# Four edits to the opening of a two-layer transformer kernel: order of weight rows, DMA transposes, finer evacuation, passes of 128 tokens

## Chip, cores, metric

One core of a Trainium2 chip. The metric is the device time of one execution in microseconds (us). The fast runs of one kernel in one group of rounds lie within 0.03 to 0.25% of each other; times are compared within rounds on one chip, fast runs only (one run of the kernel before took 3484 us and is not fast). "TensorE", "vector engine" (DVE), "ACT" and "sync engine" (SP) are the engines; SP does nothing here but issue DMAs.

## The reference

Two layers, each of attention and a gated MLP, on 2048 tokens of 1024 features in bf16:

```python
x = x + attention(layernorm(x), wqkv, wo)   # 32 heads of 32; 8 keys per token, 2 apart
x = x + w2( silu(w1 ln(x)) * (w3 ln(x)) )   # F = 3584
# and both once more with the same weights
```

`attention` projects Q, K and V by one matrix `wqkv` (1024 x 3072), gathers keys and values at 0, 2, ..., 14 tokens back, takes a softmax over 8 logits, and projects by `wo`.

## The kernel before

Tokens are worked in 4 chunks of 512. TensorE runs: Q of chunk 0 (the opening, `first_q`), K and V of chunk 0, then Q, K, V of chunks 1 to 3, with the first tiles of the output projection between the products of chunk 3, then the rest of the output projection and the MLP chunk by chunk. Attention itself has no product: the vector engine does it elementwise from transposed Q, K, V, which go through DRAM (`qkv_d`). It works in halves of 256 tokens, and its output `oT` is what the output projection takes.

The opening: x arrives in tiles of 128 tokens, is normalised, transposed by TensorE through PSUM, and multiplied by wq, which arrives in 8 rows of 256 KB. All DMAs but one are issued on the sync engine, in this order:

```python
load_tile(0, 0, 512, nc.sync);  load_tile(0, 512, D, nc.scalar)   # x tile 0
load_tile(1, 0, D, nc.sync)
loads(0, 2);  load_tile(2, 0, D, nc.sync)      # rows 0,1 of wq; x tile 2
loads(2, 4);  load_tile(3, 0, D, nc.sync)      # rows 2,3; x tile 3
loads(4, 8)          # rows 4..7, then (k1 == KT) both halves of wk and x chunk 1: 3 MB
# ... cut: statistics, normalisation, transposes, products of the four tiles
for i, acc in enumerate(accumulators(2, 2 * P)):     # tiles 2 and 3: one pass of 256 columns
    ...
    nc.sync.dma_start(q_rows[:, 2 * i:2 * i + 2, 0:CH], hT[:, 2 * i:2 * i + 2, :])  # Q to DRAM
    then[i]()        # x chunk 2; half of wv; other half of wv; x chunk 3
```

The K pass that follows, cut:

```python
for t0 in range(0, KT, SG):                       # SG = 2
    sgt = stg.tile([P, SG, CH], BF16, name="sgt") # 3 buffers
    for t in range(t0, t0 + SG):
        ...8 products of 512 columns into ps...
        background(r)                             # vector engine's work, in a fixed order
        nc.scalar.copy(sgt[:, t - t0, :], ps[:])  # ACT
    nc.sync.dma_start(qkv_d[l][which][:, t0:t0 + SG, c * CH:(c + 1) * CH], sgt[:])
```

The order of instructions on each engine is fixed when the kernel is built (in c1 below the vector engine stands idle for 2.68 us before statistics that are ahead of attention in that order). The square root of each norm is an ACT instruction between those copies, and the vector engine waits for it (6 waits, 6.1 us in all, between 20 and 165 us of the profile before):

```python
nc.vector.bn_aggr(mv[:, i, :], st[:, i, :, :])
if i == 1:
    nc.scalar.activation(sd[:], mv[:, :, 1], ACTF.Sqrt, bias=epst[:])
...
yield 0.10, at["sd"], lambda: nc.vector.reciprocal(rstd[:], sd[:])
```

And the vector engine's order is: norm of x chunk 1, statistics of x chunks 2 and 3, then attention without a break.

Of the kernel before, what the change touches and what calls it, by code (L numbers as in the profile page):

```python
# [7 lines left out]
FP32 = mybir.dt.float32  # L8
BF16 = mybir.dt.bfloat16
# [6 lines left out]
def kernel(  # L16
# [13 lines left out]
    nc = tc.nc  # L30
    cfg = dict(cfg or {})
    P = 128
    _, S, D = A_x.shape
    F = B_w1.shape[1]
    KT = D // P
    W, DIL, Dh = 8, 2, 32
    assert D == 1024 and KT == 8 and D // Dh == 32
    CH = 512
    NCH = S // CH
    TPC = CH // P  # L40
# [35 lines left out]
    psum = ctx.enter_context(tc.tile_pool(name="psum", bufs=8, space=PSUM))  # L76
# [70 lines left out]
    ident = const.tile([P, P], BF16, name="ident")  # L147
# [13 lines left out]
    hT = const.tile([P, HTN, CH], BF16, name="hT")  # L161
# [3 lines left out]
    def warm(n):  # L165
        for i in range(n):
            pw = bank("pw")
            nc.tensor.matmul(pw[:], lhsT=zero[:, 0, 0:P], rhs=zero[:, 0:2, :].rearrange("p a b -> p (a b)"),
                             start=True, stop=True)
# [8 lines left out]
    KH = KT // 2  # L178
# [51 lines left out]
    def first_q(ws, loads, then):  # L230


        xnT = xnTs["Q", 0, 0] = xtp.tile([P, KT, CH], BF16, name="xnT")
        st = small.tile([P, TPC, 2, 6], FP32, name="st1", bufs=1)
        mv = small.tile([P, TPC, 2], FP32, name="mv1", bufs=1)
        sd = small.tile([P, TPC], FP32, name="sd1", bufs=1)
        rstd = small.tile([P, TPC], FP32, name="rstd1", bufs=1)
        q_rows = qkv_d[0][0][:].rearrange("i t s -> (i t) s").rearrange("(b p) s -> p b s", p=P)

        def load_tile(j, h0, h1, queue):  # L240
            queue.dma_start(x_sb[:, j, h0:h1], xin[:, j, h0:h1])  # L241

        load_tile(0, 0, 512, nc.sync)
        load_tile(0, 512, D, nc.scalar)
        load_tile(1, 0, D, nc.sync)
        loads(0, 2)
        load_tile(2, 0, D, nc.sync)
        loads(2, 4)
        load_tile(3, 0, D, nc.sync)
        loads(4, 8)  # L250
        preload = small.tile([P, 1], FP32, name="preload", bufs=1)
        nc.scalar.activation(preload[:], epst[:], ACTF.Sqrt)

        def stats(j, hh):
            nc.vector.bn_stats(st[:, j, hh, :], x_sb[:, j, hh * 512:(hh + 1) * 512])  # L255

        def deviation(j):
            nc.vector.bn_aggr(mv[:, j, :], st[:, j, :, :])
            nc.scalar.activation(sd[:, j:j + 1], mv[:, j, 1:2], ACTF.Sqrt, bias=epst[:])  # L259

        def apply(j, parts=1):
            nc.vector.reciprocal(rstd[:, j:j + 1], sd[:, j:j + 1])
            xn = xnp.tile([P, D], BF16, name="xn")
            for i in range(parts):
                d = slice(i * D // parts, (i + 1) * D // parts)
                nc.vector.tensor_scalar(xn[:, d], x_sb[:, j, d], mv[:, j, 0:1], rstd[:, j:j + 1],  # L266
                                        op0=ALU.subtract, op1=ALU.mult)
            return xn

        def transpose(xn):  # L270
            pTs = []
            for h in range(2):
                pT = psum.tile([P, KH, P], BF16, name="pT", tag="mm")
                for kk in range(KH):
                    nc.tensor.transpose(pT[:, kk, :], xn[:, (h * KH + kk) * P:(h * KH + kk + 1) * P], ident[:])  # L275
                pTs.append(pT)
            return pTs

        def evacuate(j, h, pTs, copy):
            copy(xnT[:, h * KH:(h + 1) * KH, j * P:(j + 1) * P], pTs[h][:])  # L280

        def product(out, kk, b, tok, start, stop):
            nc.tensor.matmul(out, lhsT=ws[kk // KH][:, kk % KH, b * P:(b + 1) * P], rhs=xnT[:, kk, tok],  # L283
                             start=start, stop=stop, skip_group_check=True)

        def accumulators(per, n):
            return [psum.tile([P, per, n], FP32, name="pq", tag="mm") for _ in range(KT // per)]

        warm(NWARM)
        stats(0, 0)  # L290
        stats(0, 1)
        deviation(0)
        stats(1, 0)
        xn = apply(0, 2)
        pTs = transpose(xn)
        evacuate(0, 0, pTs, nc.scalar.copy)
        stats(1, 1)
        evacuate(0, 1, pTs, nc.vector.tensor_copy)
        deviation(1)

        accs = accumulators(4, P)
        tok = slice(0, P)

        def step0(kk):
            for b in range(KT):
                product(accs[b // 4][:, b % 4, :], kk, b, tok, kk == 0 and b % 4 == 0, kk == KT - 1)

        for kk in range(6):
            step0(kk)
        stats(2, 0)  # L310
        xn = apply(1)
        pTs = transpose(xn)
        for h in range(2):
            evacuate(1, h, pTs, nc.scalar.copy)
        for kk in range(6, KT):
            step0(kk)
        stats(2, 1)
        deviation(2)
        for i in range(2):
            nc.scalar.copy(hT[:, 4 * i:4 * i + 4, tok], accs[i][:])  # L320

        accs = accumulators(4, P)
        tok = slice(P, 2 * P)

        def block1(b):
            for kk in range(KT):
                product(accs[b // 4][:, b % 4, :], kk, b, tok, kk == 0, kk == KT - 1)
            if b % 4 == 3:
                nc.scalar.copy(hT[:, b - 3:b + 1, tok], accs[b // 4][:])

        stats(3, 0)
        xn = apply(2)
        stats(3, 1)
        deviation(3)
        for b in range(3):
            block1(b)
        pTs = transpose(xn)
        for h in range(2):
            evacuate(2, h, pTs, nc.scalar.copy)
        xn = apply(3)  # L340
        for b in range(3, 5):
            block1(b)
        pTs = transpose(xn)
        evacuate(3, 0, pTs, nc.scalar.copy)
        evacuate(3, 1, pTs, nc.vector.tensor_copy)
        for b in range(5, KT):
            block1(b)

        tok = slice(2 * P, CH)
        for i, acc in enumerate(accumulators(2, 2 * P)):  # L350
            for b in range(2):
                for kk in range(KT):
                    product(acc[:, b, :], kk, 2 * i + b, tok, kk == 0, kk == KT - 1)
            nc.scalar.copy(hT[:, 2 * i:2 * i + 2, tok], acc[:])
            nc.sync.dma_start(q_rows[:, 2 * i:2 * i + 2, 0:CH], hT[:, 2 * i:2 * i + 2, :])
            then[i]()
        qkv_at[0, 0, 0] = now["act"] + DMA / 2

    def tree(n, mul, dst):
# [144 lines left out]
    w_tiles, due, used = [], [], [0]  # L504

    def load_weight(pieces=1):

        if len(w_tiles) == len(seq):
            return
        kind, i, n, *rest = seq[len(w_tiles)]  # L510
        if kind == "qkv":
            w = wp.tile([P, KH, D], BF16, name="wqkv", tag="w")
            step = KH // pieces
            for k0 in range(0, KH, step):
                nc.sync.dma_start(w[:, k0:k0 + step, :],
                                  wqkv_v[:, n * KH + k0:n * KH + k0 + step, i * D:(i + 1) * D])
        elif kind == "w2":
            w = wp.tile([P, 8, 512], BF16, name="w2t", tag="w")
            nc.sync.dma_start(w[:, 0:n, :], w2_v[:, i:i + n, rest[0] * 512:(rest[0] + 1) * 512])
        else:  # L520
            w = wp.tile([P, KT, FG * P], BF16, name=kind + "t", tag="w")
            v = w1_v if kind == "w1" else w3_v
            nc.sync.dma_start(w[:, :, 0:n * P], v[:, :, i * P:(i + n) * P])
        w_tiles.append(w)
# [151 lines left out]
    def load_x(c):  # L676
        nc.sync.dma_start(x_sb[:, c * TPC:(c + 1) * TPC, :], xin[:, c * TPC:(c + 1) * TPC, :])
# [3 lines left out]
    def load_wq(k0, k1):  # L681
        for kk in range(k0, k1):
            nc.sync.dma_start(w_tiles[kk // KH][:, kk % KH, :], wqkv_v[:, kk, 0:D])  # L683
        if k1 == KT:
            load_weight()
            load_weight()
            load_x(1)

    first_q(w_tiles[0:2], load_wq, (lambda: load_x(2), load_weight, load_weight, lambda: load_x(3)))
    xnT_at["Q", 0, 0], norm_left["Q", 0, 0] = now["pe"], 0  # L690
    queue_norm(("Q", 0, 1), 1, 0)
    queue_norm(("Q", 0, 1), 1, 1)
# [3 lines left out]
    for c in range(NCH):  # L696
        for which in range(3):
# [4 lines left out]
            then = ()  # L702
            if c == 0 and which == 0:
                continue
            if c == 2 and which == 0:
                then = (None, None, lambda: nc.sync.dma_start(wo[:], wo_v))
            if c == 2 and which == 1:
                then = (load_weight, None, load_weight)
# [50 lines left out]
```

## Time and profile before

| | before |
|---|---|
| median of 6 runs (lowest fast) | 1618.8 us (1618.17) |
| span in the profile | 1616.3 us |
| first product of the K pass | 24.64 us |
| first attention instruction on the vector engine | 47.74 us |
| last `oT` of the first 512 tokens starts | 160.38 us |

From the page of the kernel before: span, busy time of each engine, granted TensorE clock in 40 slices (9 means 0.9 or more), and the shares of the chain of waits that ended last.

```profile
span 1616.3 us, 19263 instructions
...
PE 1610.7 (100%) x7609; PEld 805.3 (50%) x7609; DVE 1176.6 (73%) x1965; ACT 353.6 (22%) x547; POOL 1.9 (0%) x12
...
PEclk9999999999999999999999999999999999999999
...
PE 99%; DMA 0%; SPq 0%; DVE 0%; ACT 0%; issue 0%
```

TensorE is busy for the whole span, and nearly the whole chain is TensorE.

The 3 MB of wk and x chunk 1 are issued by 8.9 us. At 37.16 the first stores of K are issued. On the sync engine they stand behind two DMA transposes of x chunk 1, which both kernels have, and the issue of these ends at 37.06, about when the last load ahead of them, x chunk 3, has landed (37.18). ACT waits 3.48 us for the first of the stores, because it has to free a buffer of `sgt`; the square root behind ACT's copy (40.51) then ends a wait of 2.29 us of the vector engine (40.85). At 159.32 TensorE begins the output projection's tile that reads the last parts of `oT`, and the last part is written at 160.38 to 160.67. Below "waits", for all time after 25 us, stands this one line for TensorE (us in total, times, longest):

```profile
PEld L552 <- DVE oT L371: 0.2, 1, 0.2
```

A note on times: from here on, landings, those of the prediction too, are counted from a zero 0.12 us later than that of the timelines. The landing of x chunk 3 at 37.18 on the timelines is 37.06 there.

### The profile page before, as it was taken

Reading aid. Unit: us, or ns where it says so; the run is one execution under the profiler, and the core shown is the slowest. Engines: PE = TensorE matmul, PEld = TensorE weight load, DVE = VectorE, ACT = ScalarE, POOL = GpSimd, SP = SyncE. Lnnn points to the kernel's source line nnn. Section 1 sums busy time; section 2 is a strip of 40 time slices with the busy share of each in tenths; the row PEclk is TensorE's granted clock in tenths of the full one; section 3 lists DMA queues with packets and bytes.
Section 4 is the critical chain, followed back from the end, with each engine's and each line's share of the span. In section 5 each row is a group of like instructions: output and inputs, shape, how many; then the busy total and the mean of one; then the engine's idle time right before and its main releaser. Section 6 shows DMA issues by size and latency. Waiting matters only on the chain.

```text
span 1616.3 us, 19263 instructions
## 1 busy us (share of the span) xinstructions
PE 1610.7 (100%) x7609; PEld 805.3 (50%) x7609; DVE 1176.6 (73%) x1965; ACT 353.6 (22%) x547; POOL 1.9 (0%) x12
## 2 busy tenths in 40 slices
PE   9999999999999999999999999999999999999999
PEld 6666544444445544455444554445544444444444
DVE  5999898989899899998998449983599832222212
ACT  4433311212112230222302123021230212011110
POOL 0000000000000000000000000000000000000000
PEclk9999999999999999999999999999999999999999
DMA  9565855466537773577553776528684266436440
GB/s 314 149 190 158 254 178 169 129 193 190 170 105 236 222 203 125 169 208 249 160 186 120 211 239 175 186 97 259 210 223 158 93 194 170 143 108 218 157 130 27
DMA packets 336427, 285.82 MB, mean 177 GB/s; under 512 B 69712, under 2 KB 318928, under 8 KB 336208
## 3 DMA queue, kind: packets, MB, share of 16 engines
q1 hardware_dynamic: 336192, 284.46, 58.0%
q8 instruction: 59, 0.97, 0.2%
q14 instruction: 32, 0.26, 0.0%
q10 hardware_dynamic: 144, 0.13, 0.0%
HBM read 239.47 MB, written 29.36 MB: 166 GB/s over the span
## 4 chain that ended last, share of the span: by engine, by line
PE 99%; DMA 0%; SPq 0%; DVE 0%; ACT 0%; issue 0%
PE acc L658 24%; PE pu L642 24%; PE pg L634 24%; PE ps L591 20%; PE po L552 7%; PE pq L283 1%; DMA wqkv<-in_A_wqkv_dram 0%; SPq L683 0%; SPq L241 0%; DVE xn L266 0%; ACT xnT L280 0%; PE pT L275 0%; DVE st L255 0%; ACT sd L259 0%; DVE x_sb L668 0%
## 5 line engine op out<-in xcount | busy, mean ns | idle before, releaser
L642 PE MATMUL pu<-xnT,w3t 128*128 128x512 bf16 x1792 | 423.4, 379 | 0.0
L634 PE MATMUL pg<-xnT,w1t 128*128 128x512 bf16 x1792 | 423.4, 379 | 0.0
L658 PE MATMUL acc<-w2t,hT 128*128 128x512 bf16 (+1 forms) x1804 | 389.7, 378 | 0.0
L591 PE MATMUL ps<-xnT,wqkv 128*128 128x512 bf16 x1472 | 319.2, 379 | 0.0
L638 ACT ACTIVATE sg<-pg 128x512 bf16<-128x512 f32 x224 | 133.6, 597 | 773.0 <-PE pg L634 719.4
L646 DVE TENSOR_TENSOR hT<-sg,pu 128x512 bf16<-128x512 bf16 x224 | 152.6, 681 | 186.8 <-PE pu L642 177.8
L658 PEld LDWEIGHTS <-hT 128*128 128x128 bf16 x1804 | 176.5, 98 | 210.5
L642 PEld LDWEIGHTS <-w3t 128*128 128x128 bf16 x1792 | 175.4, 98 | 211.4
L634 PEld LDWEIGHTS <-w1t 128*128 128x128 bf16 x1792 | 175.3, 98 | 211.4
L591 PEld LDWEIGHTS <-wqkv 128*128 128x128 bf16 x1472 | 211.1, 143 | 106.7
L424 DVE TENSOR_TENSOR pr<-qT,kT 128x2048 bf16<-128x2048 bf16 x128 | 156.2, 1221 | 87.2 <-DMA kT<-qkv_d 85.1
L668 DVE TENSOR_TENSOR x_sb<-x_sb,acc 128x512 bf16<-128x512 bf16 x129 | 87.3, 677 | 107.6 <-PE acc L658 107.4
L484 DVE TENSOR_TENSOR tm<-At,vT 128x2048 bf16<-128x2048 bf16 x128 | 156.1, 1220 | 2.4
L595 ACT CAST sgt<-ps 128x512 bf16<-128x512 f32 x184 | 106.7, 585 | 230.7 <-PE ps L591 211.9
L369 DVE TENSOR_TENSOR tm<-tm 128x1024 bf16<-128x1024 bf16 (+1 forms) x256 | 134.5, 550 | 0.4
L369 DVE TENSOR_TENSOR pr<-pr 128x1024 bf16<-128x1024 bf16 (+1 forms) x256 | 134.0, 551 | 0.5
L552 PE MATMUL po<-wo,oT 128*128 128x512 bf16 x512 | 115.7, 379 | 0.0
L552 PEld LDWEIGHTS <-oT 128*128 128x128 bf16 x512 | 50.1, 98 | 60.1 <-DVE oT L371 0.2
L189 DVE BATCH_NORM_STATS2 st<-x_sb 128x6 f32<-128x512 bf16 x120 | 75.9, 671 | 4.6 <-DMA x_sb<-in_A_x_dram 4.6
L557 DVE TENSOR_TENSOR x_sb<-x_sb,po 128x512 bf16<-128x512 bf16 x64 | 43.3, 684 | 19.2 <-PE po L552 18.9
L638 ACT ACT_TABLE_LOAD x31 | 39.8, 1283 | 51.2 <-PE pg L634 51.0
L446 DVE STREAM_TRANSPOSE psmT<-psm 128x2048 bf16<-128x2048 bf16 x16 | 36.9, 2306 | 0.2
(85 smaller groups left out, 402.3 us busy)
## 6 DMA issues: line engine op xcount, KB each, us to landing
w1t<-in_B_w_dram SPq DMA_DIRECT2D x56, 1024.0 KB, 5.5
w3t<-in_B_w_dram SPq DMA_DIRECT2D x56, 1024.0 KB, 8.0
w2t<-in_B_w_dram SPq DMA_DIRECT2D x48, 1024.0 KB, 5.4
wqkv<-in_A_wqkv_dram SPq DMA_DIRECT2D x28, 1024.0 KB, 6.8
qkv_d<-sgt SPq DMA_DIRECT2D x92, 256.0 KB, 2.9
qT<-qkv_d SPq DMA_DIRECT2D x16, 512.0 KB, 8.4
w2t<-in_B_w_dram SPq DMA_DIRECT2D x16, 512.0 KB, 5.2
kT<-qkv_d SPq DMA_DIRECT2D x14, 544.0 KB, 9.5
```

Of the source, the lines that this page charges most:

```text
L369: nc.vector.tensor_tensor(b[:, 0:m, :], b[:, 0:m, :], b[:, m:2 * m, :], op=ALU.add)
L424: V.tensor_tensor(pr[:], qT[:], kT[:, :, k0:k0 + TCH], op=ALU.mult)
L484: V.tensor_tensor(tm[:], At[:], win, op=ALU.mult)
L552: nc.tensor.matmul(ps[:], lhsT=oT[:, t, j * P:(j + 1) * P], rhs=wo[:, t, hh * 512:(hh + 1) * 512], start=(t == 0), stop=(t == KT - 1))
L591: nc.tensor.matmul(ps[:], lhsT=ws[kk // KH][:, kk % KH, t::KT], rhs=xnT[:, kk, :], start=(kk == 0), stop=(kk == KT - 1))
L595: nc.scalar.copy(sgt[:, t - t0, :], ps[:])
L634: nc.tensor.matmul(pg[:], lhsT=w1t[:, kk, fi * P:(fi + 1) * P], rhs=xnT[:, kk, :], start=(kk == 0), stop=(kk == KT - 1))
L638: nc.scalar.activation(sg[:], pg[:], ACTF.Silu)
L642: nc.tensor.matmul(pu[:], lhsT=w3t[:, kk, fi * P:(fi + 1) * P], rhs=xnT[:, kk, :], start=(kk == 0), stop=(kk == KT - 1))
L646: nc.vector.tensor_tensor(hT[:, f - f0, :], sg[:], pu[:], op=ALU.mult)
L658: nc.tensor.matmul(acc[:], lhsT=hT[:, f - f0, j * P:(j + 1) * P], rhs=w2ts[(f - f0) // 8][:, (f - f0) % 8, q0:q0 + step], start=(f == f0), ...
L668: nc.vector.tensor_tensor(xs, xs, acc[:], op=ALU.add)
```

## The change

Its intent is to start the products of the opening sooner and keep TensorE free of transposes:

1. rows of wq load ahead of x tiles 2 and 3;
2. tiles 2 and 3 are transposed by DMA, not by TensorE and ACT;
3. the first tile's transposes are evacuated in pieces of 2, 2 and 4 blocks instead of 4 and 4;
4. tiles 2 and 3 are multiplied in two passes of 128 columns instead of one of 256.

The loads of wk and x chunk 1 move with it: they are now issued inside tile 1's pass, which on the sync engine is behind both DMA transposes.

```diff
         load_tile(1, 0, D, nc.sync)
-        loads(0, 2)
+        loads(0, 4)
         load_tile(2, 0, D, nc.sync)
-        loads(2, 4)
+        loads(4, 8)
         load_tile(3, 0, D, nc.sync)
-        loads(4, 8)
 ...
+        def transpose_dma(j, xn):
+            nc.sync.dma_start_transpose(out=xnT[:, :, j * P:(j + 1) * P], in_=xn[:])
 ...
-        pTs = transpose(xn)
-        evacuate(0, 0, pTs, nc.scalar.copy)
+        p0, p1, p2 = transpose(xn, (0, 2, 4, 8))
+        evacuate(0, p0, nc.scalar.copy)
+        evacuate(0, p1, nc.scalar.copy)
 ...
+        transpose_dma(2, xn)
 ...
+        transpose_dma(3, xn)
+
+        for j in range(1, TPC):
+            for i, acc in enumerate(accumulators()):
+                for b in range(4):
+                    for kk in range(KT):
+                        product(j, acc[:, b, :], kk, 4 * i + b, kk == 0)
+                keep(j, i, acc)
+                if j == 1 and i == 0:
+                    then[0]()                  # wk, x chunk 1
+                if j == TPC - 1:
+                    nc.sync.dma_start(q_rows[:, 4 * i:4 * i + 4, 0:CH], hT[:, 4 * i:4 * i + 4, :])
+                    then[1 + i]()              # x chunk 2, wv; wv, x chunk 3
 ...
-        if k1 == KT:
-            load_weight()
-            load_weight()
-            load_x(1)
```

More of the change, by code (lines that the diff above doesn't have):

```diff
@@ L268, in apply, with transpose, evacuate, product @@
             return xn
-        def transpose(xn):
+        def transpose(xn, cuts):
             pTs = []
-            for h in range(2):
-                pT = psum.tile([P, KH, P], BF16, name="pT", tag="mm")
-                for kk in range(KH):
-                    nc.tensor.transpose(pT[:, kk, :], xn[:, (h * KH + kk) * P:(h * KH + kk + 1) * P], ident[:])
-                pTs.append(pT)
-            return pTs
-        def evacuate(j, h, pTs, copy):
-            copy(xnT[:, h * KH:(h + 1) * KH, j * P:(j + 1) * P], pTs[h][:])
-        def product(out, kk, b, tok, start, stop):
-            nc.tensor.matmul(out, lhsT=ws[kk // KH][:, kk % KH, b * P:(b + 1) * P], rhs=xnT[:, kk, tok],
-                             start=start, stop=stop, skip_group_check=True)
-        def accumulators(per, n):
-            return [psum.tile([P, per, n], FP32, name="pq", tag="mm") for _ in range(KT // per)]
+            for k0, k1 in zip(cuts, cuts[1:]):
+                pT = psum.tile([P, k1 - k0, P], BF16, name="pT", tag="mm")
+                for kk in range(k0, k1):
+                    nc.tensor.transpose(pT[:, kk - k0, :], xn[:, kk * P:(kk + 1) * P], ident[:])
+                pTs.append((k0, k1, pT))
+            return pTs
+        def evacuate(j, part, copy):
+            k0, k1, pT = part
+            copy(xnT[:, k0:k1, j * P:(j + 1) * P], pT[:])
+        def transpose_dma(j, xn):
+            nc.sync.dma_start_transpose(out=xnT[:, :, j * P:(j + 1) * P], in_=xn[:])
+        def product(j, out, kk, b, start):
+            nc.tensor.matmul(out, lhsT=ws[kk // KH][:, kk % KH, b * P:(b + 1) * P],
+                             rhs=xnT[:, kk, j * P:(j + 1) * P], start=start, stop=kk == KT - 1,
+                             skip_group_check=True)
+        def accumulators():
+            return [psum.tile([P, 4, P], FP32, name="pq", tag="mm") for _ in range(2)]
+        def keep(j, i, acc):
+            nc.scalar.copy(hT[:, 4 * i:4 * i + 4, j * P:(j + 1) * P], acc[:])
         warm(NWARM)
@@ L294, in first_q @@
         xn = apply(0, 2)
-        pTs = transpose(xn)
-        evacuate(0, 0, pTs, nc.scalar.copy)
+        p0, p1, p2 = transpose(xn, (0, 2, 4, 8))
+        evacuate(0, p0, nc.scalar.copy)
+        evacuate(0, p1, nc.scalar.copy)
         stats(1, 1)
-        evacuate(0, 1, pTs, nc.vector.tensor_copy)
+        evacuate(0, p2, nc.vector.tensor_copy)
         deviation(1)
-        accs = accumulators(4, P)
-        tok = slice(0, P)
-        def step0(kk):
-            for b in range(KT):
-                product(accs[b // 4][:, b % 4, :], kk, b, tok, kk == 0 and b % 4 == 0, kk == KT - 1)
@@ L308, in first_q @@
-        for kk in range(6):
-            step0(kk)
         stats(2, 0)
         xn = apply(1)
-        pTs = transpose(xn)
-        for h in range(2):
-            evacuate(1, h, pTs, nc.scalar.copy)
-        for kk in range(6, KT):
-            step0(kk)
         stats(2, 1)
         deviation(2)
-        for i in range(2):
-            nc.scalar.copy(hT[:, 4 * i:4 * i + 4, tok], accs[i][:])
-        accs = accumulators(4, P)
-        tok = slice(P, 2 * P)
-        def block1(b):
-            for kk in range(KT):
-                product(accs[b // 4][:, b % 4, :], kk, b, tok, kk == 0, kk == KT - 1)
-            if b % 4 == 3:
-                nc.scalar.copy(hT[:, b - 3:b + 1, tok], accs[b // 4][:])
+        accs = accumulators()
@@ L331, in first_q @@
+        for kk in range(KT):
+            for b in range(KT):
+                product(0, accs[b // 4][:, b % 4, :], kk, b, kk == 0 and b % 4 == 0)
+            if kk == 4:
+                p0, p1 = transpose(xn, (0, 4, 8))
+        evacuate(1, p0, nc.scalar.copy)
+        evacuate(1, p1, nc.scalar.copy)
         stats(3, 0)
         xn = apply(2)
+        transpose_dma(2, xn)
         stats(3, 1)
         deviation(3)
-        for b in range(3):
-            block1(b)
-        pTs = transpose(xn)
@@ L338, in first_q @@
-        for h in range(2):
-            evacuate(2, h, pTs, nc.scalar.copy)
-        xn = apply(3)
-        for b in range(3, 5):
-            block1(b)
-        pTs = transpose(xn)
-        evacuate(3, 0, pTs, nc.scalar.copy)
-        evacuate(3, 1, pTs, nc.vector.tensor_copy)
-        for b in range(5, KT):
-            block1(b)
-        tok = slice(2 * P, CH)
-        for i, acc in enumerate(accumulators(2, 2 * P)):
-            for b in range(2):
-                for kk in range(KT):
-                    product(acc[:, b, :], kk, 2 * i + b, tok, kk == 0, kk == KT - 1)
-            nc.scalar.copy(hT[:, 2 * i:2 * i + 2, tok], acc[:])
-            nc.sync.dma_start(q_rows[:, 2 * i:2 * i + 2, 0:CH], hT[:, 2 * i:2 * i + 2, :])
-            then[i]()
+        for i in range(2):
+            keep(0, i, accs[i])
@@ new lines, in first_q @@
+        xn = apply(3)
+        transpose_dma(3, xn)
+        for j in range(1, TPC):
+            for i, acc in enumerate(accumulators()):
+                for b in range(4):
+                    for kk in range(KT):
+                        product(j, acc[:, b, :], kk, 4 * i + b, kk == 0)
[5 more added lines that the diff above has]
+                    then[1 + i]()
@@ L683, in load_wq, with load_k, load_v0, load_v1 @@
             nc.sync.dma_start(w_tiles[kk // KH][:, kk % KH, :], wqkv_v[:, kk, 0:D])
-        if k1 == KT:
-            load_weight()
-            load_weight()
-            load_x(1)
-    first_q(w_tiles[0:2], load_wq, (lambda: load_x(2), load_weight, load_weight, lambda: load_x(3)))
+    def load_k():
+        load_weight()
+        load_weight()
+        load_x(1)
+    def load_v0():
+        load_x(2)
+        load_weight()
+    def load_v1():
+        load_weight()
+        load_x(3)
+    first_q(w_tiles[0:2], load_wq, (load_k, load_v0, load_v1))
     xnT_at["Q", 0, 0], norm_left["Q", 0, 0] = now["pe"], 0
```

## The prediction

> **What bounds it now.** TensorE. The page has PE busy 1610.7 of a 1616.3 us span (100%), clock 1.000, and the chain of waits that ended last is 99% PE. The list of waits after 25 us shows 0.2 us of PE waiting in all: once the first 128x512 product of the K pass starts (24.64 us, timeline) TensorE streams without a hole for 1591.7 us. The change touches only what comes before: its worth is the shift of that start, plus any new hole. Two per cent (32 us) exceeds the whole prologue.
>
> **The prologue before** (timeline, chain of waits). First transposes at 6.28, first product 7.35 behind a 0.58 us evacuation of 512 columns on ACT. The first tile's pass is paced by rows of wq: holes of 0.24, 0.87 and 0.23 us on the weight load, each ended by a wq DMA. From the records of landings, pieces of 256 KB land about 0.66 us apart in issue order: row 3 at 8.8, row 4 at 10.1, row 7 at 12.1. The tile's pass ends near 12.7, tile 1's with the transposes of tiles 2 and 3 (about 0.45 us of PE each, plus 0.29 waiting for xn) near 17.7, then 64 products of 256 columns at 0.109 us = 7.0 us.
>
> The gap of warm products[...]: 0.056 us at 128 columns, 0.216 at 512 in this trace.
>
> **What the change does** (estimates from those durations).
> - Finer evacuation: the first copy is 256 columns (0.38 us as the cast of that size on ACT) after two transposes instead of four: first product at about 7.05, -0.3. Row 4 of wq then paces the pass: mostly lost in a wait.
> - Rows ahead of x tiles: rows 4 to 7 land one slot (0.66 us) earlier, row 7 at about 11.4. x tile 2 lands at 8.8 instead of 7.1, and its statistics stand ahead of tile 1's normalisation on DVE: xn of tile 1 at 10.3, its transposes wait about 0.3. Tile 0 ends near 12.1. The sqrt for tile 2 stands ahead of tile 1's evacuations on ACT: another 0.2-0.3 us hole. Tile 1 ends near 16.0, with no transposes inside it: 1.7 us ahead of before.
> - DMA transposes: x tile 3 still lands at 12.1; its first statistics, then xn of tile 2 at 13.65. A DMA transpose takes 1.29 us to issue and at least 3.1 (median 3.3) from issue to landing, so tile 2 is ready at about 16.9. TensorE waits about 1 us. Tile 3 (18.9) is in time.
> - Passes of 128 tokens: 128x0.056 = 7.2 instead of 7.0, +0.2.
> The K pass starts at about 24.2 instead of 24.64.
>
> **What it may cost.** The loads of wk and x chunk 1 now queue behind the transposes on the sync engine: issued at 17.0 instead of 7.3, wk's second half lands at about 24-24.6 (2.7 us per MB); it is needed at 25.0. wv's second half lands near 37.6, needed at 38.9. Either can make a hole of up to 1 us; expected 0.2.
>
> **Predicted:** 1618.4 us (-0.3), range 1616.9 to 1619.9; faster by 2% 0.005, within 0.985, slower 0.01.
>
> **Right or wrong, in the profile:** first product near 7.05; tile 0's products ending near 12.1; a TensorE wait of 1 us before tile 2's products, ended by the DMA transpose; first 128x512 product at 24.2.
>
> **What would make it wrong:** a DMA transpose quicker than 3.1 us in the quiet queue (gain up to 1 us more); wk landing behind the transposes by 1-2 us (loss); a slow run (3484 us).

The spacings are measured: 56 ns from start to start at 128 columns, 109 at 256 and 216 at 512 (medians in the profile before). The forecast's sum: 0.44 us gained at the start of the K pass (24.2 instead of 24.64), 0.2 expected to be lost in holes, recorded as -0.3 and 1618.4 us.

## More of the kernel before

The timeline of the kernel before (start, duration, engine, line, operation, output<-input, count, and in brackets how long the engine idled and what ended it):

```profile
7.25 1.32 SPq L515 DMA_DIRECT2D wqkv<-in_A_wqkv_dram  x2
8.90 0.37 SPq L677 DMA_DIRECT2D x_sb<-in_A_x_dram  x1
...
21.57 1.29 DVE L189 BATCH_NORM_STATS2 st<-x_sb 128x6 f32<-128x512 bf16 x2 [4.56 <-DMA x_sb<-in_A_x_dram]
...
24.64 35.56 PE L591 MATMUL ps<-xnT,wqkv 128*128 128x512 bf16 x164
...
26.94 10.12 SPq L217 DMA_TRANSPOSE xnT<-xn  x2
37.16 1.04 SPq L600 DMA_DIRECT2D qkv_d<-sgt  x2
...
39.76 0.59 ACT L595 CAST sgt<-ps 128x512 bf16<-128x512 f32 x1 [3.48 <-DMA qkv_d<-sgt]
...
40.51 0.31 ACT L194 ACTIVATE sd<-mv,epst 128x2 f32<-128x2 f32 x1
...
40.85 0.17 DVE L201 RECIPROCAL rstd<-sd 128x2 f32<-128x2 f32 x1 [2.29 <-ACT sd L194]
...
47.74 1.21 DVE L424 TENSOR_TENSOR pr<-qT,kT 128x2048 bf16<-128x2048 bf16 x1
...
159.32 3.62 PE L552 MATMUL po<-wo,oT 128*128 128x512 bf16 x16
...
160.38 0.29 DVE L371 TENSOR_TENSOR oT<-tm 128x256 bf16<-128x256 bf16 x1
```

## The result

| | before | after |
|---|---|---|
| median (6 runs each) | 1618.8 us | 1626.68 us |
| ratio of fast runs | | 1.0047 (95%: 1.0033 to 1.0061) |
| span in the profile | 1616.3 | 1624.3 |
| mean granted clock | 1.000 | 0.998 |
| first K product | 24.64 | 23.86 |
| K pass runs without a hole from | 24.64 | 26.36 |
| first attention instruction | 47.74 | 54.02 |
| last `oT` of the first 512 tokens starts | 160.38 | 166.66 |

A ratio is the mean time of one kernel's fast runs over that of the other's in the same rounds, so it is not quite the ratio of the medians quoted. The change is 8 us slower: within 2%, but clear of noise and far outside the predicted range. From the page of the kernel after:

```profile
span 1624.3 us, 19357 instructions
...
PE 1613.1 (99%) x7657; PEld 805.9 (50%) x7657; DVE 1176.5 (72%) x1964; ACT 350.5 (22%) x545; POOL 1.9 (0%) x12
...
PEclk9999999999999999999999999999999999999999
...
PE 90%; DVE 8%; DMA 2%; SPq 0%; issue 0%; ACT 0%; ACTq 0%; DVEq 0%
```

Now 8% of the chain is the vector engine: about 130 us in which TensorE is busy and yet not what the end waits for. The slices are too coarse to show the clock. The timeline of the kernel after, the lines that answer to those of before and the new waits:

```profile
13.49 3.19 SPq L283 DMA_TRANSPOSE xnT<-xn  x2
...
16.71 7.32 PE L286 MATMUL pq<-xnT,wqkv 128*128 128x128 bf16 x128 [0.86 <-DMA xnT<-xn]
16.73 1.15 SPq L500 DMA_DIRECT2D wqkv<-in_A_wqkv_dram  x2
17.92 0.51 SPq L662 DMA_DIRECT2D x_sb<-in_A_x_dram  x1
...
23.86 1.03 PE L576 MATMUL ps<-xnT,wqkv 128*128 128x512 bf16 x4
...
26.36 33.89 PE L576 MATMUL ps<-xnT,wqkv 128*128 128x512 bf16 x156 [1.46 <-DMA wqkv<-in_A_wqkv_dram]
...
28.99 1.29 DVE L189 BATCH_NORM_STATS2 st<-x_sb 128x6 f32<-128x512 bf16 x2 [13.50 <-DMA x_sb<-in_A_x_dram]
...
33.05 9.29 SPq L217 DMA_TRANSPOSE xnT<-xn  x2
42.43 1.05 SPq L585 DMA_DIRECT2D qkv_d<-sgt  x2
...
46.03 0.59 ACT L580 CAST sgt<-ps 128x512 bf16<-128x512 f32 x1 [4.18 <-DMA qkv_d<-sgt]
...
46.78 0.31 ACT L194 ACTIVATE sd<-mv,epst 128x2 f32<-128x2 f32 x1
...
47.12 0.17 DVE L201 RECIPROCAL rstd<-sd 128x2 f32<-128x2 f32 x1 [2.99 <-ACT sd L194]
...
54.02 1.20 DVE L409 TENSOR_TENSOR pr<-qT,kT 128x2048 bf16<-128x2048 bf16 x1
...
160.24 1.24 PE L537 MATMUL po<-wo,oT 128*128 128x512 bf16 x5
163.95 0.61 PE L537 MATMUL po<-wo,oT 128*128 128x512 bf16 x1 [2.47 <-DVE oT L356]
166.34 4.50 PE L537 MATMUL po<-wo,oT 128*128 128x512 bf16 x10 [1.79 <-DVE oT L356]
...
166.66 0.29 DVE L356 TENSOR_TENSOR oT<-tm 128x256 bf16<-128x256 bf16 x1
```

The opening went nearly as predicted: the wait for the transpose is 0.86 us, and the first K product comes 0.8 us sooner. Then wk is late (1.46 us), x chunk 1 is 7.4 us late, the two DMA transposes ahead of K's first store are issued by 42.34 instead of 37.06, the store is 6.3 us late at ACT (46.03 against 39.76), the square root behind it as late at the vector engine (47.12 against 40.85), attention starts 6.3 us late (54.02 against 47.74), and `oT` is 6.3 us late more than 100 us further on (166.66 against 160.38). There TensorE stands. The stretches around it (length, busy us and instructions of PE, PEld, DVE, ACT, POOL, then granted clock, DMA share, GB/s):

```profile
160.00:164.00 4.00, 1.53 (x8) 0.55 (x6) 3.89 (x10) 2.72 (x6) 0.00 (x0) 0.96 0.20 68
164.00:168.00 4.00, 2.16 (x5) 0.58 (x6) 3.97 (x7) 0.00 (x0) 0.00 (x0) 0.50 0.94 201
168.00:172.00 4.00, 4.00 (x15) 1.80 (x13) 2.49 (x5) 0.00 (x0) 0.00 (x0) 0.68 0.96 294
```

The clock falls to 0.50 after the hole, at 163.70, and stays there for 6.83 us by the clock records, while TensorE has work again. In other runs below the stretch is 3.4 us long (e1, e3) or 6.8 us (e4, d4). When it fell here, TensorE had been idle for 2.22 us (since 161.48) and had worked for 1.24 us before that (from 160.24).

The sum from the profiles: the vector engine 6.28 us late (166.66 - 160.38), and from there to the end 1457.6 us instead of 1455.9 (spans less those times), 1.7 us more. Together 8.0, the difference of the spans. What TensorE's opening gained or lost does not appear in this sum: it is swallowed in the wait.

### The profile page after: what moved, and what is told of

It reads as the page before. It is cut to its first block, busy times and chain, and to the rows that moved or that the text cites. A ratio compares the mean times of both kernels' runs of the same rounds, so it can differ in the third digit from the quotient of the medians.

```text
span 1624.3 us, 19357 instructions
## 1 busy us (share of the span) xinstructions
PE 1613.1 (99%) x7657; PEld 805.9 (50%) x7657; DVE 1176.5 (72%) x1964; ACT 350.5 (22%) x545; POOL 1.9 (0%) x12
## 4 chain that ended last, share of the span: by engine, by line
PE 90%; DVE 8%; DMA 2%; SPq 0%; issue 0%; ACT 0%; ACTq 0%; DVEq 0%
PE acc L643 24%; PE pu L627 24%; PE pg L619 24%; PE ps L576 12%; PE po L537 6%; DVE pr L409 1%; DVE tm L469 1%; DMA x_sb<-in_A_x_dram 1%; DVE tm L354 1%; DVE pr L354 1%; DVE st L189 1%; DVE xn L214 0%; DVE At L453 0%; DMA wqkv<-in_A_wqkv_dram 0%; DVE L L433 0%; DVE psmT L431 0%
## 5 line engine op out<-in xcount | busy, mean ns | idle before, releaser
L537 PEld LDWEIGHTS <-oT 128*128 128x128 bf16 x512 | 50.4, 99 | 66.5 <-DVE oT L356 5.8
```

The source lines that it names most:

```text
L537: nc.tensor.matmul(ps[:], lhsT=oT[:, t, j * P:(j + 1) * P], rhs=wo[:, t, hh * 512:(hh + 1) * 512], start=(t == 0), stop=(t == KT - 1))
```

## The experiments

The theory after reading: the loads behind the transposes come late, which makes the vector engine late, and the vector engine has no slack at 160 us. Which landing holds it was open. Theory A: that of x chunk 1. Theory B: the whole queue is late, and the first store of K is what counts, since ACT waits for it and the square roots stand behind ACT's copy. Rival R: the shorter passes and the new wait in the opening cost it by themselves. Landings below are from the trace's landing records, with the zero named above.

### e1: x chunk 1 ahead of the transposes

```diff
         load_tile(3, 0, D, nc.sync)
+        load_x(1)
 ...          (in then[0])
         load_weight()
         load_weight()
-        load_x(1)
```

> The changed kernel with one move: the 1 MB load of x chunk 1 is issued before the two DMA transposes instead of behind them and behind wk. Theory A (the lateness on the vector engine comes from the late landing of x chunk 1, 28.8 us against 21.4): attention starts at 47.7 us as before, no hole near 160 us, time 1619.6 (the K pass still loses 0.9 on wk). Theory B (the whole queue is late, and what counts is the landing of the first store of K, 45.8 against 39.5, which holds ACT and behind it the square roots that the vector engine waits for): x lands by 17 us, but 5 MB still stand between wk and that store, which lands at about 42.9; attention starts about 3.4 us late, the hole near 160 us stays at about 3 us, time 1622. Rival R (the shorter passes and the wait for the transpose cost it by themselves): no change, 1626.7.

Measured: 1623.77 us (ratio 1.0032, 1.0019 to 1.0046). x chunk 1 landed at 14.6 us, 14 us sooner than in the changed kernel, yet the first store of K landed at 43.55, attention started at 51.75, 4.0 us late, and TensorE waited 3.0 us for `oT`. Theory A falls, and so does R as the whole cause; B holds, with 4.0 us where 3.4 was expected, and 1623.77 where 1622 was.

### e2: all 3 MB ahead of the transposes

```diff
         load_tile(3, 0, D, nc.sync)
+        then[0]()
 ...
-                if j == 1 and i == 0:
-                    then[0]()
```

> The changed kernel with wk and x chunk 1 (3 MB) issued before the DMA transposes, as early as in the kernel before. The transposes then stand behind 3 MB in the queue: tile 2 ready at 22 us instead of 16.7, first K product at 29.5 instead of 23.9, no hole on wk. Theory A: x chunk 1 in time, so the vector engine is in time at 160 us and the time is that of the K pass's start, about 1623.5. Theory B: the store of Q, and with it everything behind it, goes out at 28 us, the first store of K lands at about 46, as late as in the changed kernel: about 1626.

Measured: 1632.18 us (1.0081). The transposes landed at 22.8 us behind the loads, TensorE waited 6.8 us for tile 2, then ran at half clock for a part of the next 128 products (9.88 us in all, 7.32 in the changed kernel), and the K pass began at 32.64. The first store of K landed at 51.9 and attention started at 60.09. Worse than both expectations (the half clock was not foreseen), in the direction of B. x chunk 1 was in time (21.9), so once more it is not what counts.

### e3: TensorE transposes tiles 2 and 3 again

```diff
-        transpose_dma(2, xn)
+        xn2 = xn
-        transpose_dma(3, xn)
 ...          (in tile 1's pass, after blocks 2 and 6; then[0]() moved up as in e2)
+                    if j == 1 and 4 * i + b in (2, 6):
+                        jj, src = (2, xn2) if 4 * i + b == 2 else (3, xn)
+                        for part in transpose(src, (0, 4, 8)):
+                            evacuate(jj, part, nc.scalar.copy)
```

> The changed kernel with tiles 2 and 3 transposed by TensorE again (inside tile 1's pass), and wk and x chunk 1 therefore issued right behind the rows of wq, as before. Rows ahead, finer pieces and four passes stay. First K product at 23.7 us (1 us ahead of before). Theory A: vector engine in time, about 1618. Theory B: the first store of Q is now 512 KB and leaves 2 us later than the first of 256 KB before, so the queue is 1 to 2 us late: first store of K at about 41, time 1619.5 to 1620.5. Rival R: still near 1626.

Measured: 1622.97 us (1.0022, 1.0009 to 1.0034). Half of the loss is gone, not all: neither R's 1626 nor A's 1618, and above B's 1619.5 to 1620.5, with the half clock for 3.4 us after the hole. The loads of wk and x chunk 1 landed as before (19.3 and 21.9), but Q's first store, now of 512 KB, was issued at 23.44 us instead of 20.21, and everything behind it followed late: first store of K at 43.29 (expected 41), attention at 51.50. So the passes of 128 tokens do cost something, but through the store that waits for the last pass, not through TensorE.

### e4: the kernel before with x chunk 1 late

```diff
             load_weight()
             load_weight()
-            load_x(1)
 ...
-(lambda: load_x(2), load_weight, load_weight, lambda: load_x(3))
+(lambda: (load_x(1), load_x(2)), load_weight, load_weight, lambda: load_x(3))
```

> The kernel before with one move: the load of x chunk 1 is issued behind the first store of Q (20 us) instead of at 8.9 us. TensorE's prologue does not change: first K product at 24.6. Both theories on the queue: everything behind lands one megabyte, 2.65 us, later (first store of K 42.2 instead of 39.5), attention starts 2.6 late, TensorE meets a hole of 2.6 us near 160 us: 1621.4. Rival R: no change, 1618.8.

Measured: 1621.46 us (1.0021, 1.0009 to 1.0034), runs from 1621.16 to 1624.76. TensorE's opening is untouched, and a hole near 160 us appears with none of the change's four edits. The timeline of e4, TensorE:

```profile
161.68 0.39 PE L552 MATMUL po<-wo,oT 128*128 128x512 bf16 x1 [0.65 <-DVE oT L371]
164.08 4.68 PE L552 MATMUL po<-wo,oT 128*128 128x512 bf16 x10 [2.01 <-DVE oT L371]
```

In the profiled run attention started 4.0 us late (expected 2.6), and the half clock followed for 6.8 us; that is the run of 1624.76. This is the cleanest evidence that late loads alone cost the time. What is left of R falls with c4 below, which keeps the passes of 128 and loses nothing.

### c1 and c2: x chunk 3 behind the first store of K

In the changed kernel (c1) and in the kernel before (c2) the last load of the opening moves behind the first store of K:

```diff
-        load_x(3)                     (in the opening)
+            if c == 0 and which == 1:
+                then = (lambda: load_x(3),)   (behind K's first store)
```

> The changed kernel with the last of the prologue's loads, 1 MB of x chunk 3, issued behind the first store of K instead of ahead of it. Nothing in TensorE's prologue changes (transpose wait 0.9, hole on wk 1.5). If the landing of the first store of K sets the vector engine's time, it lands 2.65 us earlier (43.2), attention starts at 51.4, and the hole near 160 us shrinks by as much: about 1623.5. If the late landing of x chunk 1 (28.8 us, not touched here) sets it, nothing changes: 1626.7.

Measured c1: 1626.7 us (1.005): nothing gained, where 1623.5 was expected. The store did land at 42.95, as expected, and ACT's wait for it shrank to 1.3 us; but now x chunk 3 landed at 47.26, and the vector engine, whose order puts the statistics of chunk 3 ahead of attention, waited for that:

```profile
47.41 1.29 DVE L189 BATCH_NORM_STATS2 st<-x_sb 128x6 f32<-128x512 bf16 x2 [2.68 <-DMA x_sb<-in_A_x_dram]
```

The expected time was wrong: one late landing replaced another. So B in its narrow form (the store alone) falls; what is late is the stream of DMAs, and several landings on it can be the last one.

> The same move in the kernel before. First store of K at 36.9 instead of 39.5, attention starts at about 45.1 instead of 47.7, so the vector engine is 2.6 us ahead at 160 us, where TensorE did not wait for it: time unchanged, 1618.7. If the time falls by 2 us, then TensorE was not the limit there and the reading of before is wrong.

Measured c2: 1618.15 us (0.9999, 0.9985 to 1.0012), unchanged as expected, but attention started at 48.00, not at 45.1, for the same reason (x chunk 3 landed at 41.02). It therefore did not test what more slack on the vector engine does.

### c3: products of no use in the hole

```diff
+            fill = {5: 14, 6: 8}
             for t in range(KT):
+                for _ in range(fill.get(t, 0)):      # this one tile only
+                    nc.tensor.matmul(pw[:], lhsT=wo[:, 0, 0:P], rhs=wo[:, 0, 0:512], start=True, stop=True)
```

> The changed kernel with 22 products of no use (14 ahead of the sixth product of the output tile that waits, 8 ahead of the seventh; 4.7 us of TensorE at full clock) put into the hole near 160 us. The vector engine is as late as in the changed kernel (attention at 54.0, last part of oT at 166.9). If part of the loss is the half clock that follows the hole, the clock stays at 1.0 there and the time falls by 1.7 to 2 us, to about 1625; if the clock is only a by-product, it stays at 1626.7 or rises.

Measured: 1624.51 us (1.0039, against 1626.68 and 1.0047 for the changed kernel, in another group of rounds; c1, with the same loss and in the same rounds as c3, had 1626.7, and its fastest run, 1625.94, is slower than the slowest of c3, 1625.56). The timeline of c3, TensorE, and below it the stretch that ran at half clock in the changed kernel:

```profile
162.16 3.19 PE L542 MATMUL pw<-wo 128*128 128x512 bf16 x14
165.18 0.38 PE L543 MATMUL po<-wo,oT 128*128 128x512 bf16 x1
165.40 1.89 PE L542 MATMUL pw<-wo 128*128 128x512 bf16 x8
167.56 0.39 PE L543 MATMUL po<-wo,oT 128*128 128x512 bf16 x1 [0.27 <-DVE oT L356]
```

```profile
164.00:168.00 4.00, 3.68 (x17) 1.29 (x14) 3.93 (x9) 0.52 (x2) 0.00 (x0) 1.00 0.81 172
```

The clock stays at 1.00. In this profile the vector engine was even later (last `oT` starts at 167.87), but from there to the end it is 1455.9 us, the same as in the kernel before and 1.7 less than after. So the half clock is a real part of the loss, 1.7 us, and the rest is the wait.

### c4: loads that wait for nothing, TensorE transposes

e3, and additionally:

```diff
     def load_k():
         load_weight()
         load_weight()
         load_x(1)
+        load_x(2)
+        load_weight()
+        load_weight()
 ...          (load_v0 and load_v1 empty; x chunk 3 behind K's first store)
```

> The changed kernel's rows ahead, finer pieces and four passes, with TensorE transposing tiles 2 and 3, and with wk, x chunk 1, x chunk 2 and wv all issued right behind the rows of wq, x chunk 3 behind the first store of K. The queue has no gap at 19 to 21 us, the first store of K lands at about 34, no later than in the kernel before, attention starts before 47.7: no hole near 160, and the time is that of the K pass's start, 0.3 to 0.8 us ahead of before: 1618.2. If it is still above 1620, something other than the queue makes the parts that it keeps slow.

Measured: 1617.41 us (0.9994, 0.9981 to 1.0006); all five runs between 1617.12 and 1617.91. First store of K at 36.7 (expected 34), x chunk 3 at 39.54, attention at 46.52, and TensorE's list of waits shows nothing after 25 us. Three of the four edits are kept here, and the loss is gone. By the medians it is 1.4 us faster than the kernel before and 9 us faster than the changed one; against the kernel before the interval includes 1.

### d1: c4 with one pass of 256 columns for tiles 2 and 3

```diff
-        for j in range(1, TPC):
+        for j in range(1, 2):            # tile 1 alone
+        for i in range(4):               # then tiles 2 and 3, 256 columns, as before
```

> The kernel with the early loads (c4), with tiles 2 and 3 again in one pass of 256 columns. From the spacings of the kernel before (0.109 us at 256 columns against 0.056 at 128): the Q pass ends 0.2 us sooner, 1617.2; if the four passes were worth anything for tiles 2 and 3, it gets slower. Resolution of the times is about 0.5 us, so the spacing in the profile decides.

Measured: 1618.08 us (0.9995), c4 and d1 not being on the same chip. From the first product to the first K product it took 17.50 us (7.54 to 25.04) against 17.33 in c4 (7.10 to 24.43): a pass over both tiles has to wait for tile 3's transposes (0.77 us in the profile), which gives back what the wider products save. The expected gain of 0.2 us was not there; the number of passes is worth nothing either way.

### d2 and d3: single edits in the kernel before

d2 has the rows ahead only (loads 0 to 3, x tile 2, loads 4 to 7, x tile 3, then wk as before); d3 has the cuts (0, 2, 4, 8) for the first tile only.

> The kernel before with the rows of wq ahead of x tiles 2 and 3 and nothing else. Tile 0's pass ends up to 0.7 us sooner, the first K product comes 0.3 to 0.6 us sooner, but the first store of K, and the vector engine at 160 us, are where they were (39.5; 160.7), so TensorE gives the gain back there in a short wait: 1618.6, same within noise. If the time falls by the whole gain, the vector engine is not a second limit of the kernel before.

Measured d2: 1618.65 us (1.0000, 0.9987 to 1.0012). First K product at 24.51, only 0.1 sooner (17.11 us after the first product, against 17.29 before). TensorE then waited 1.1 us for `oT` near 160 us. The time is as expected, the gain in the opening was smaller (0.2 us, not 0.3 to 0.6), and in this profile another landing was the last: the third store of K, at 48.01, attention at 49.13.

> The kernel before with the first tile's transposes evacuated in three pieces and nothing else. First product 0.25 us sooner, then given back in the waits for rows of wq: first K product at most 0.1 us sooner, time unchanged, 1618.8.

Measured d3: 1619.16 us (1.0001), 16.97 us from first product to first K product, 0.5 us of waiting for `oT` near 160. Its first product came no sooner (7.40, against 7.35 before) and its first K product 0.3 us sooner (24.37), where 0.25 and at most 0.1 were expected; profiles with the same opening as before (before, c2, e4) have 7.35 to 7.86 and 24.64 to 25.10, so neither difference is clear of the spread. Neither edit alone costs or gains anything measurable.

### d4: the DMA transposes kept, another order of loads

```diff
         load_tile(3, 0, D, nc.sync)
+        load_weight()                    # first half of wk, ahead of the transposes
 ...          (then[0], behind the transposes)
         load_weight()
-        load_weight()
         load_x(1)
+        load_x(2)
+        load_weight()
+        load_weight()
 ...          (x chunk 3 behind K's first store)
```

> The changed kernel, DMA transposes kept, with another order of loads alone: first half of wk ahead of the transposes (it fills the idle queue), behind them the second half, x chunk 1, x chunk 2 and wv without waiting for the stores of Q, x chunk 3 behind the first store of K. From the runs so far attention starts at the latest of: first store of K landed plus 8.2; x chunk 3 landed plus 7.0; x chunk 1 landed plus 22.6. Estimated landings 37, 39.6, 23.7: attention at 46.6, no hole near 160. Transposes land 0.4 later than in the changed kernel, no hole on wk: first K product at 24.3. Time 1618.3, that is the whole loss of 8 us gone by order alone. If it stays above 1622, the DMA transposes cost something that the rule lacks.

Measured: 1625.14 us (1.0038, 1.0024 to 1.0052): the expectation failed. The opening was the best: the timeline of d4, TensorE,

```profile
16.69 7.32 PE L287 MATMUL pq<-xnT,wqkv 128*128 128x128 bf16 x128 [1.06 <-DMA xnT<-xn]
23.85 6.43 PE L577 MATMUL ps<-xnT,wqkv 128*128 128x512 bf16 x29
```

with no hole on wk. But x chunk 1 landed at 26.2 (expected 23.7) and x chunk 3 at 44.98 (expected 39.6), attention started at 51.96, and the hole of 4.1 us near 160 remained, with the half clock. The rule (landing of x chunk 3 plus 7.0) gave the start to 0.02 us; my estimate of the landings was wrong, because one megabyte does not fill the time that the queue loses around the transposes: in d4's DMA view the slices between 13.9 and 19.3 us move 0 to 290 GB/s, those after, to 25 us, 307 to 423.

### f1 and f2: loads from ACT's queue

Left open by d4: do the loads land late because they are issued behind the transposes, or because of what the transposes do to the DMA engines? f1 issues wk, x chunks 1 to 3 and wv from ACT, beginning at 11 us, before the transposes; f2 leaves the first half of wk on the sync queue ahead of them and issues the rest from ACT at 14.7 us.

```diff
-        load_weight(); load_weight(); load_x(1)                         (nc.sync)
+        load_weight(queue=nc.scalar); load_weight(queue=nc.scalar); load_x(1, nc.scalar)
 ...          (x chunks 2 and 3 and wv likewise; the calls moved up)
```

> The changed kernel, DMA transposes kept on the sync queue, with all 7 MB of later loads issued from ACT's queue: wk and x chunk 1 at about 12.3 us, the rest at about 16. The DMA engines work through the time in which they stood idle; the transposes share them and land up to 1 us later (first K product 24.0 to 24.8); wk, x chunks 1 and 3 land at about 19, 22 and 33, and the stores of K no longer stand behind loads. If order is the cause: attention before 47.7, no hole near 160 us, 1617.8 to 1618.8. If the transposes themselves cost it: 1622 or more.

> The same with the first half of wk on the sync queue ahead of the transposes and everything else from ACT at about 16.4 us, when the second transpose is under way. Transposes as in the changed kernel (first K product 23.9), x chunk 1 at about 24, x chunk 3 at about 36. If order is the cause: attention at 43 to 47, no hole, 1617.5 to 1618.3. If the transposes themselves cost it: 1622 or more.

Measured: f1 1628.75 us (1.0062, 1.0048 to 1.0076), f2 1624.7 us (1.0036, 1.0023 to 1.0048). By the time alone the second outcome came (1622 or more), but not by the path that I had in mind: that the transposes would land up to 1 us later beside the loads was an estimate of mine that no run had shown, and in f1 they landed 8.7 and 13.0 us later. The hole near 160 us is gone in both, and the whole loss is in the opening: the K pass begins at 35.11 (f1) and 31.32 (f2) instead of 24.64, 10.5 and 6.7 us late, and the spans are as much longer (1626.9 and 1623.1). The timeline of f1, TensorE:

```profile
25.34 4.99 PE L286 MATMUL pq<-xnT,wqkv 128*128 128x128 bf16 x64 [9.59 <-DMA xnT<-xn]
31.53 3.75 PE L286 MATMUL pq<-xnT,wqkv 128*128 128x128 bf16 x64 [1.20 <-DMA xnT<-xn]
35.11 5.14 PE L576 MATMUL ps<-xnT,wqkv 128*128 128x512 bf16 x22
```

and its DMA view for 19 to 24 us, packets and MB of ACT's queue (q10) and of the sync engine's (q1), which in this stretch holds the transposes alone:

```profile
q10 hardware_dynamic: 835, 1.67, 88.9%
q1 hardware_dynamic: 834, 0.21, 18.9%
```

In these 5 us the two queues moved packets in equal numbers, 834 against 835. A packet of a load has 2048 bytes, one of a transpose 256, so the transposes got 11% of the bytes; the first landed at 25.2 us and the second at 31.4, instead of 16.5 and 18.4.

So the question was wrongly put as an alternative. Behind the loads the transposes come late (e2: 22.8 us); ahead of the loads they leave the queue idle while it waits for the normalised tile (the changed kernel: the last row of wq and x tile 3 landed by 12.0, the queue moved 6 GB/s from 12.0 to 14.7, and the loads of 2048-byte packets flowed again from about 18; of those 6 us the two transposes themselves move data for about 3); side by side they come late as well (TensorE waited 10.8 us for them in f1, 6.4 in f2). In this opening, where the next 7 MB are all wanted, no place that I tried for them was free.

### Eleven of the profiles against one rule

Attention starts at the latest of: first store of K landed plus 8.2 us; third store of K landed plus 1.1; x chunk 3 landed plus 7.0 (with landings on the timeline's zero: 8.1, 1.0 and 6.9). The constants are read off these profiles; the first and the last were on record before d1 to d4 ran, and d1 and d4 kept to the last within 0.02 us. The last `oT` starts 112.6 to 112.7 us after that in every row, because the vector engine has almost no waits in between (1.4 us in the kernel before from 20 to 165 us on ACT's exponentials). c2, d1 and d3, not listed, obey it too; f1 and f2 do not: attention starts at 56.36 and 52.56, later than any of the three landings asks for (52.6 and 50.4 at the latest), so a late K pass is a limit that the rule lacks; it is hidden there, since TensorE is later still and does not wait near 160 us.

| profile | K runs from | first K store | x chunk 3 | attention starts | set by | last oT starts | to the end |
|---|---|---|---|---|---|---|---|
| before | 24.64 | 39.54 | 37.06 | 47.74 | 1st store | 160.38 | 1455.9 |
| after | 26.36 | 45.81 | 42.35 | 54.02 | 1st store | 166.66 | 1457.6 |
| e1 | 25.84 | 43.55 | 41.08 | 51.75 | 1st store | 164.40 | 1457.6 |
| e2 | 32.64 | 51.88 | 49.43 | 60.09 | 1st store | 172.75 | 1458.6 |
| e3 | 24.41 | 43.29 | 40.95 | 51.50 | 1st store | 164.17 | 1457.2 |
| e4 | 25.10 | 43.09 | 40.63 | 51.73 | 3rd store (50.61) | 164.39 | 1458.6 |
| c1 | 26.41 | 42.95 | 47.26 | 54.24 | x chunk 3 | 166.92 | 1458.1 |
| c3 | 27.21 | 46.99 | 43.44 | 55.20 | 1st store | 167.87 | 1455.9 |
| c4 | 24.43 | 36.68 | 39.54 | 46.52 | x chunk 3 | 159.18 | 1456.9 |
| d2 | 24.51 | 40.06 | 37.53 | 49.13 | 3rd store (48.01) | 161.78 | 1455.9 |
| d4 | 23.85 | 41.44 | 44.98 | 51.96 | x chunk 3 | 164.61 | 1458.4 |

"To the end" is the span less the last column but one. It is 1455.9 where the vector engine binds without a fall of the clock, 1457.2 to 1458.6 where the half clock followed, and 1456.9 in c4, where TensorE binds and the vector engine is ahead.

## Why the prediction was wrong

Point by point:

- "First product at about 7.05": 7.44 in the profile of after; 6.94 to 7.59, median 7.10, in the ten other runs with the same code there. In the profile of after the warm-up products ran longer (13 in 5.68 us, 5.05 before) and the transposes began behind them, at 6.70. Right in the middle and wide in the spread, and without weight: rows of wq pace the pass (1.3 us of waits for them in the profile before, 0.3 after).
- "Tile 0's products ending near 12.1": the last of them runs from 11.95 to 12.16. Right; tile 1's end at 15.84, where 16.0 was estimated.
- "TensorE waits about 1 us" for the DMA transpose, "at least 3.1" us to landing: 0.86 us, and 3.1. Right.
- "The K pass starts at about 24.2": 23.86, and 24.26 and 24.99 in c1 and c3, which have the same opening. Right within the jitter.
- "wk's second half lands at about 24-24.6 ... expected 0.2": it landed at 26.19 and made a hole of 1.46 us. The mechanism was named, the size was not: I had costed 2.7 us per MB from the issue and the transposes, but data of wk flowed only from about 18 us. wv's second half, expected at 37.6, landed at 39.87, just before its first use at 40.2: no hole.
- "The change touches only what comes before: its worth is the shift of that start, plus any new hole." This is the step that failed. I read the span after 24.64 us as a fixed 1591.7 us because TensorE streams there, and looked for new holes only where TensorE takes the loads itself, in wk and wv. The holes came at 160 us, from the vector engine, and e4 shows that late loads make one with TensorE's opening untouched. The line of 0.2 us of waiting, which I quoted as proof that nothing else binds, was the sign of a second chain that arrives at the same time.
- Not in the prediction at all: the half clock after the hole, 1.7 us (c3).

The sum that should have stood there: x chunk 1 and all later DMAs about 6 us late, because their issue moves from 7.3 to 16.7 us and the queue has no rest after 21.5 us in which to catch up (341 GB/s from there to 37 us in the profile before, 100 in the 2.5 us ahead of it); attention late by the same; slack at 160 us 0.2 us; loss about 6 us, and more if the clock falls. Every number of it was in the profile before, apart from the clock.

What was not settled: why attention's lateness in e4 was 4.0 us in the profile while the fastest runs of e4 lost only 2.5; the landings vary from run to run, and only profiled runs show them. And whether c4 truly beats the kernel before: 5 runs say 0.06%, with an interval that includes nothing gained.

## What to carry to other kernels

A TensorE that is busy 100% of the time does not show that nothing else binds (here it was 100% busy, and late loads alone cost 2.6 us in e4): look for the places where it takes another engine's output with a wait near zero (0.2 us here), and follow that engine back to the first landing it depends on. When a change puts an instruction that waits on a computed value into the queue that issues loads, cost the delay of everything behind it, to the end of the backlog (here the issue of wk moved by 9.5 us, and attention came 6.3 us late). If a DMA transpose must share the queue with loads that are wanted at once, check the three places it can have (ahead, behind, beside; here 1625.14 us in d4, 1632.18 in e2, 1624.7 in f2) against simply letting TensorE do it (1617.41 in c4).

## Clock and DMA transpose, as measured here

- The clock fell to 0.50 in e3 and e4 although no single wait was longer than 2.01 us (two waits, of 1.12 or 0.65 and 2.01 us, with one product between them). In the 4 us from 160 to 164 TensorE was busy for 1.53 us in the changed kernel, 1.42 in e4, 1.34 in e1 and 0.39 in d4, and the mean clock of the 4 us after was 0.50, 0.50, 0.72 and 0.50; in d2 (2.91 us busy, longest wait 0.82) and c3 (4.00 busy) it stayed at 1.00. Whether it goes by the length of a wait or by the share of work, these runs do not tell.
- In the changed kernel, in an otherwise idle queue, the first transpose of 128 x 1024 bf16 moved about 210 GB/s (189 to 225 in the slices between 14.9 and 16.1 us). From issue to landing it took 3.1 us, of which 1.3 is issue.
- f1, with a transpose next to ordinary loads, gave correct results; in time, beside a stream of loads from another queue, the landing went from 3.1 us to a median of 14.0 (f1), with as many packets as the load but 256 bytes in each against 2048.
